# Attention and expert layer on one core: full rows in the middle slot's transfers, GpSimd's work in source order, table scatters a step behind the ranks

## The chip, the cores and the metric

The kernel runs on one core of one Trainium2 chip. The metric is device time in microseconds (us), the median of several executions. The engines are named as the profile names them: PE is TensorE (PEld its weight loads), DVE is VectorE, ACT is ScalarE, POOL is GpSimd, SP is SyncE, whose queue issues most DMAs. POOL issues the indirect ones.

## The reference

Eight batches of eight heads with 576 tokens each; the attention keeps only scores within `tau` of a row's maximum. Its output, 4608 tokens of 512 values, goes through a layer of eight experts, of which each token takes one.

```python
scores = scale * np.matmul(q, k.transpose(0, 1, 3, 2))        # q, k, v: (8, 8, 576, 64)
thresh = np.max(scores, axis=-1, keepdims=True) - tau
scores = np.where(scores >= thresh, scores, -1000000000.0)
attn = softmax(scores)                                        # sum + 1e-9
x = (attn @ v).transpose(0, 2, 1, 3).reshape(4608, 512)

logits = x @ w_gate + modality_bias[modality_id]
e_idx = np.argmax(logits, axis=1)
gate_w = softmax(logits)[range(N), e_idx]
for e in range(8):
    mask = e_idx == e
    h = np.maximum(x[mask] @ w1[e], 0.0)                      # w1[e]: 512 x 1024
    out[mask] = gate_w[mask, None] * (h @ w2[e])              # w2[e]: 1024 x 512
```

## The kernel before

Two heads make a pair; there are 32 pairs of nine steps each, one step for a tile of 128 queries (four tiles for each head, and one for the last 64 queries of both). In a step PE computes scores (L369), DVE takes the negated maximum `nm` (L386), ACT the exponentials `e` (L392), DVE the masked product `pr` (L404); two steps later PE transposes `pr` (L420), and later in the pair multiplies by `v` (L458).

Products of full precision are made of two parts each: an operand is split into a rounded part and the rest. `prep_steps` prepares the next pair in steps 0, 1 and 2 of a pair: PE transposes the remainder and the main rows of k and q (L294, L311), ACT copies them to `str` and `st` (L298, L299, L314), and POOL splits them in `split_pool` (a cast at L282, a subtraction at L283) into `nk`, `qb` and `nq`. SP then moves the halves to `km` (L320) and `q` (L323), from which the next pair's scores read. A weight block is loaded by SP into `raw` (four buffers; L771 for `w1`, L775 for `w2`) and split by POOL into `w1h`, `w1l` or `w2h`, `w2l` (L790 and L792; three buffers for `w1`, five for `w2`).

A "slot" is up to 512 tokens of one expert. Beside the attention run two slots of 256 and five of 512 (`SIDE`), each as soon as enough batches are done: `route_a` and `route_b` rank the tokens of a batch by expert, POOL scatters token number and gate weight to `tab` in five indirect DMAs (L617), `pick` chooses the expert, SP reads the slot's rows of the table to `tb` (L735), POOL gathers the tokens' rows to `xg` (L747), PE transposes them (L761) and computes the two layers (L805, L832), and POOL scatters the result `y` to the output (L847). After the attention follow slots for what is left (`last_slot`), in the sizes 512, 320 and 256; at least one of each of the two smaller ones always runs. The 320 are the "middle" size: two tiles of 128 rows and one of 64, `TP(t)` rows each.

Work is recorded step by step. `at(t, f)` puts a function at a step (fractions order them), `put(n, f)` behind a step's softmax, and the loop at L1053 runs them. The table `C` holds the places: for a 512-token slot, `wS`/`wL` give the steps of the weight splits, and each load stands `wl` = 3.5 steps ahead of its split. On PE the order recorded is the order run:

```python
    with tc.manual_schedule(engines={ET.PE}):
```

On the other engines a scheduler puts the instructions in an order of its own by modelled times; what stands in an engine's program then runs strictly in that order.

Of the kernel before, what the change touches and what calls it, by code (L numbers as in the profile page):

```python
# [11 lines left out]
F32 = mybir.dt.float32  # L12
# [3 lines left out]
U32 = mybir.dt.uint32  # L16
# [3 lines left out]
ET = mybir.EngineType  # L20
# [9 lines left out]
def tile_attn_moe(  # L30
# [11 lines left out]
    out: bass.AP,  # L42
):

    C = {'prep': [0, 1, 2], 'tr0': 6, 'pv0': 7, 'tr1': 12, 'sums': 13, 'pv1': 13, 'x': 14, 'gate': [15, 16, 17, 18], 'route': 18, 'routeb': 21, 'E0': 28, 'L0': 4, 'pick': -14, 'vld': 6, 'qkld': -3, 'pre': 2.5, 'wl': 3.5, 'rows': -11, 'gat': [-9.5, -8.5, -5, -4], 'xt': [-6, -5, -2, -1], 'lc': 21, 't3': 84, 'neg': 1.0, 'draw': [2, 2, 2, 2, 1, 2, 2, 1, 2], 'last': 36, 'te': 8, 'warm': 24,
         'wS': [-6, -4.7, -3.4, 3, 12.5, 14, 15.5, 21.5, 4.2, 5.4, 6.6, 7.5, 22.7, 23.8, 24.9, 25.8],
         'wL': [-5.5, -4, -2.5, 2.7, 12, 13.3, 14.6, 21, 3.8, 4.9, 6, 7.1, 15.8, 22.2, 23.4, 24.6], 'ask': 4, 'exp': -12.5, 'two': 98, 'early': []}
    nc = tc.nc
# [2 lines left out]
    DM = H * D  # L51
    DF = w1.shape[2]
    N = B * S
    P = 128
# [8 lines left out]
    W = 512  # L63
# [23 lines left out]
    xp = ctx.enter_context(tc.tile_pool(name="xp", bufs=1))  # L87
    actx = ctx.enter_context(ExitStack())
    ld = actx.enter_context(tc.tile_pool(name="ld", bufs=1))
    prep = actx.enter_context(tc.tile_pool(name="prep", bufs=1))  # L90
# [51 lines left out]
    warm = glob.tile([P, 1], F32, name="warm")  # L142
# [48 lines left out]
    xs = dram.tile([N, DM], F32, name="xs")  # L191
# [370 lines left out]


    prev_scatter = []

    def route_a(b):
        lg = state.pop(("lg", b))
# [20 lines left out]
    def route_b(b):  # L588
        l, oh = state.pop(("route", b))
        shp = [P, NT, NE]  # L590

        rk = tbank()
        rkv = rk[:, 0:(NT + 1) * NE].rearrange("p (t e) -> p t e", e=NE)
        mm(rkv, ltri, oh, True, False)
        for t in range(NT):
            mm(rkv[:, t + 1:NT + 1, :], ones_bf, oh[:, t:t + 1, :].to_broadcast([P, NT - t, NE]),
               False, t == NT - 1)

        nc.scalar.activation(out=l, in_=l, func=AF.Exp)
        pos = small.tile([P, NT + 1, NE], F32, name="pos", bufs=1)  # L600
        nc.vector.tensor_tensor(out=pos, in0=rkv, in1=base.unsqueeze(1).to_broadcast([P, NT + 1, NE]),
                                op=ALU.add)
        nc.vector.tensor_copy(out=base, in_=pos[:, NT, :])
        nc.vector.tensor_tensor(out=pos[:, 0:NT, :], in0=pos[:, 0:NT, :],
                                in1=creg.unsqueeze(1).to_broadcast(shp), op=ALU.add)
        nc.vector.tensor_tensor(out=pos[:, 0:NT, :], in0=pos[:, 0:NT, :], in1=oh[:, 0:NT, :], op=ALU.mult)
        posi = small.tile([P, NT], I32, name="posi")
        posf = small.tile([P, NT], F32, name="posf", bufs=1)
        nc.vector.tensor_reduce(out=posf, in_=pos[:, 0:NT, :], axis=AX.X, op=ALU.add)
        nc.vector.memset(posf[0:P - R, NC:NT], float(TROWS))  # L610
        nc.vector.tensor_copy(out=posi, in_=posf)
        gs = small.tile([P, NT], F32, name="gs", bufs=1)
        nc.vector.tensor_reduce(out=gs, in_=l, axis=AX.X, op=ALU.add)
        nc.vector.tensor_scalar(out=gs, in0=gs, scalar1=1e-9, scalar2=None, op0=ALU.add)
        nc.vector.reciprocal(out=pay[:, b, :, 1].bitcast(F32), in_=gs)
        for t in range(NT):
            i = _inst(nc.gpsimd.indirect_dma_start(  # L617
                out=tab, out_offset=bass.IndirectOffsetOnAxis(ap=posi[:, t:t + 1].bitcast(U32), axis=0),
                in_=pay[:, b, t, :], in_offset=None, bounds_check=TROWS - 1, oob_is_err=False))
            for o in prev_scatter:  # L620
                tc.declare_no_dep(i, o, reason="every token has a row of its own")
            prev_scatter.append(i)
# [91 lines left out]
    def slot(where, group, nrow, WT=W, wq=lambda: wp, nbuf=(4, 3, 5), lo_eng=None, xq=None):  # L714
# [3 lines left out]
        box = {}  # L718
# [3 lines left out]
        def TP(t):  # L722

            return min(P, WT - t * P)
# [17 lines left out]
        def gather(t):  # L742
            def f():
                xg = xt_pool().tile([P, DM], F32, name="xg", bufs=nx[1])
                box[("xg", t)] = xg

                nc.gpsimd.indirect_dma_start(  # L747
                    out=xg[0:TP(t)], out_offset=None, in_=xs[0:nrow, :],
                    in_offset=bass.IndirectOffsetOnAxis(ap=box["tb"][0:TP(t), t, 0:1].bitcast(U32), axis=0),
                    bounds_check=nrow - 1, oob_is_err=False)  # L750
            return f

# [68 lines left out]
        def l2(g, t, z):  # L821
            def f():
                if z == 0:
                    box["ps"] = group()
                nt = TP(t)
                ps = box["ps"]
                ts = slice(t * P, (t + 1) * P)
                f_ = g * F2 + z
                hh, hl = box[("h", f_)]
                wh, wl = box[("w", 2, f_)]  # L830
                for y, (h, w) in enumerate(((hh, wh), (hh, wl), (hl, wh))):
                    nc.tensor.matmul(out=ps, lhsT=h[:, ts], rhs=w, start=(z == 0 and y == 0),  # L832
                                     stop=(z == F2 - 1 and y == 2))
                if z < F2 - 1:
                    return
                let_go(ps)
                ps = ps[0:nt]
                tb = box["tb"][0:nt]
                if g == 0:
                    y0 = xp.tile([P, DM], F32, name="y0", bufs=W // P)[0:nt]  # L840
                    nc.scalar.activation(out=y0, in_=ps, func=AF.Copy, scale=tb[:, t, 1:2].bitcast(F32))
                    box[("y0", t)] = y0
                    return
                y = xp.tile([P, DM], F32, name="y", bufs=2)[0:nt]
                nc.vector.scalar_tensor_tensor(out=y, in0=ps, scalar=tb[:, t, 1:2].bitcast(F32),  # L845
                                               in1=box.pop(("y0", t)), op0=ALU.mult, op1=ALU.add)
                i = _inst(nc.gpsimd.indirect_dma_start(  # L847
                    out=out, out_offset=bass.IndirectOffsetOnAxis(ap=tb[:, t, 0:1].bitcast(U32), axis=0),
                    in_=y, in_offset=None, bounds_check=N - 1, oob_is_err=False))
                for o in prev_out:  # L850
                    tc.declare_no_dep(i, o, reason="every token has a row of its own")
                prev_out.append(i)
            return f
# [3 lines left out]
        ta = TT if xq else 0  # L857
        wl = C['wl']
        tb_ = ta + F2 * u1
# [9 lines left out]
        for f_ in range(FC):  # L869
# [3 lines left out]
            pre = C['pre'] if xq else C['pre'] * u1 / 2  # L873
# [28 lines left out]
    def at(t, f):  # L902
        events.setdefault(t, []).append(f)
# [32 lines left out]
    draw = [0] * (NSTEP + 2)  # L936
# [28 lines left out]
    for n0, (w, nb) in zip(begins, SIDE):  # L965
# [22 lines left out]
        for e in ev:  # L988

            if e[0] is None:  # L990
                t = n0 + e[2]
            elif n0 in begins[:-1]:

                which, f_ = e[3]
                t = n0 + C['w' + 'SL'[w == W]][8 * which + f_ - 8] - e[2]
            else:
                t = when(e[0]) - e[2]
# [24 lines left out]
        clear(fin["xp"], 4)  # L1022

    XF = NSTEP - NI + C['routeb'] + 1.5
    F0 = XF + 9.5
    at(XF, finish)

    def ask():
# [1 line left out]
    at(F0 + C['ask'], ask)  # L1030
    t0 = F0
    for z in range(3):
# [11 lines left out]
                f()  # L1044

    LAG = 2
    with tc.manual_schedule(engines={ET.PE}):

        ps = tbank()
        for _ in range(C['warm']):  # L1050
            nc.tensor.matmul(out=ps[:, 0:P], lhsT=zero, rhs=zero, start=True, stop=True, skip_group_check=True)
        prep_first(0)
        for n in range(NSTEP + LAG):  # L1053
            m = draw[n]
            if n == C['lc']:
                late_constants()
            if n == C['lc'] + 6:
                clear(xp, 2)
            two = 2 <= n < C['two']
            if n < NSTEP:  # L1060
                for hf in range(2):
                    qk_half(n, hf)
                softmax_a(n, two)
            if n == 0:
                prep_first(1)
            run_events(n - 0.5, n + 0.5)
            if two:
                if n % 2:
                    softmax_b(n - 1, two)
                    softmax_b(n, two)  # L1070
                if n >= LAG:
                    tr(n - LAG)
                if n % 2:
                    for y in (n - 1, n):
                        for f in extra.pop(y, []):
                            f()
                        pieces(draw[y])
                continue
            pieces(min(m, 1))
            if n < NSTEP:  # L1080
                softmax_b(n, two)
            if 0 <= n - LAG < NSTEP:
                tr(n - LAG)
            pieces(min(m - 1, 1))
            for f in extra.pop(n, []):
                f()
            pieces(m - 2)
# [48 lines left out]
```

## Time and profile before

| | |
|---|---|
| median of 3 runs | 1117.74 us (1115.88 to 1118.3) |
| the profiled execution | 1116.18 us |
| its span, first to last instruction | 1114.5 us |
| mean granted PE clock | 0.976 |
| busy: PE, DVE, ACT, POOL | 1029.7, 725.7, 641.9, 537.9 us |
| the last six score matmuls (L369) | from 887.08 us |

In a row of an engine's order of time stand start and duration in us, engine, line, operation, what it writes and reads, its shape, how many such instructions follow each other, and in brackets how long the engine stood idle before it, and what ended that. A row of a table of groups gives the busy time and the mean of one in ns.

### The profile page before, as it was taken

What the parts mean: (1) busy time and instruction counts of PE and PEld (TensorE: products, weight loads), DVE (VectorE), ACT (ScalarE), POOL (GpSimd) and SP (SyncE); (2) the same over time, 40 slices, a digit from 0 to 9 for tenths busy, and PEclk for the clock granted to TensorE, in tenths of its full rate; (3) what the DMA queues carried; (4) which work ended last, traced back from release to release, by engine and by line L of the source; (5) the groups of instructions that cost most, each with busy time, mean ns of one, the idle gap of its engine ahead of it and who ended that gap; (6) DMA issues with size and microseconds to landing.
All of it is one profiled execution on the core that took longest, in us unless ns stands there. A gap on an engine that the chain in (4) does not pass through costs nothing.

```text
span 1114.5 us, 20778 instructions
## 1 busy us (share of the span) xinstructions
PE 1029.7 (92%) x6683; PEld 809.9 (73%) x6683; DVE 725.7 (65%) x1773; ACT 641.9 (58%) x1474; POOL 537.9 (48%) x727
## 2 busy tenths in 40 slices
PE   7799869989798989999999999999999997999993
PEld 6676647777676767787777777777767775788883
DVE  6788857787568756876676766776677645243441
ACT  5687657666565656666666666566656523434440
POOL 2232345464655563665355644565265546442440
PEclk8999989999899999999999999999999999999997
DMA  5656557656666757476635763676465214644330
GB/s 123 140 136 160 124 128 184 165 110 165 165 161 130 180 129 184 102 202 162 168 82 141 197 161 91 148 206 147 107 141 152 97 39 134 216 145 131 131 99 21
DMA packets 212646, 156.06 MB, mean 140 GB/s; under 512 B 100782, under 2 KB 172462, under 8 KB 212528
## 3 DMA queue, kind: packets, MB, share of 16 engines
q1 hardware_dynamic: 205392, 135.72, 49.1%
q0 software_dynamic: 7136, 18.92, 5.2%
q8 instruction: 55, 0.90, 0.3%
q14 instruction: 63, 0.52, 0.1%
HBM read 84.12 MB, written 19.35 MB: 93 GB/s over the span
## 4 chain that ended last, share of the span: by engine, by line
PE 57%; DVE 3%; issue 2%; DMA 2%; ACT 1%; POOL 1%; another core or an unknown queue 0%; POOLq 0%; ACTq 0%; SPq 0%
PE bk L458 8%; PE bk L832 8%; PE bk L805 8%; PE s L369 8%; PE pm L832 7%; PE pm L805 6%; PE bk L420 6%; PE bk L761 1%; PE bk L311 1%; DVE pr L404 1%; PE bk L449 1%; DVE nm L386 1%; ACT e L392 1%; DMA xg<-xs,tb 1%; PE bk L507 1%
## 5 line engine op out<-in xcount | busy, mean ns | idle before, releaser
L386 DVE TENSOR_REDUCE nm<-s 128x1 f32<-128x576 f32 x288 | 216.9, 754 | 135.1 <-PE s L369 125.2
L392 ACT ACTIVATE e<-s,nm 128x576 f32<-128x576 f32 x288 | 215.0, 747 | 113.8 <-DVE nm L386 107.2
L404 DVE SCALAR_TENSOR_TENSOR pr<-s,nm,e 128x576 f32<-128x576 f32 x288 | 231.5, 815 | 75.1 <-ACT e L392 67.4
L369 PE MATMUL s<-km,q 128*128 128x288 f32 x1024 | 202.3, 320 | 41.1 <-DMA q<-nq 17.2
L431 ACT COPY ptm<-bk 128x512 f32<-128x512 f32 x256 | 149.3, 584 | 78.4 <-PE bk L420 66.4
L369 PEld LDWEIGHTS s<-km,q 128*128 128x128 f32 x1024 | 148.5, 192 | 62.1 <-issue 33.5
L420 PE MATMUL bk<-ident,pr 128*128 128x128 f32 x1152 | 175.8, 276 | 3.9 <-ACT ptm L431 2.0
L420 PEld LDWEIGHTS bk<-ident,pr 128*128 128x128 f32 x1152 | 143.6, 142 | 27.9 <-DVE hl L816 3.0
L458 PE MATMUL bk<-ptm,v_m 128*64 128x320 f32 (+1 forms) x1024 | 144.5, 420 | 0.1
L792 POOL TENSOR_TENSOR w2l<-raw,w2h 128x512 fp32r<-128x512 f32 x88 | 113.7, 1299 | 30.9 <-ACT w2h L788 26.7
L458 PEld LDWEIGHTS bk<-ptm,v_m 128*64 128x64 f32 x1024 | 67.6, 139 | 50.1 <-issue 10.3
L790 POOL CAST w2h<-raw 128x512 fp32r<-128x512 f32 x56 | 34.2, 613 | 140.1 <-DMA raw<-in_moe_w_dram 71.1
L433 ACT COPY rp<-pr 128x64 f32<-128x64 f32 x256 | 59.3, 248 | 56.5 <-DVE pr L404 47.0
L805 PE MATMUL bk<-xh,w1h 128*128 128x512 f32 (+1 forms) x212 | 85.5, 403 | 1.1 <-ACT xh L272 0.9
L805 PE MATMUL bk<-xl,w1h 128*128 128x512 f32 (+1 forms) x212 | 77.3, 365 | 1.9 <-DVE xl L273 1.9
L805 PE MATMUL bk<-xh,w1l 128*128 128x512 f32 (+1 forms) x212 | 76.9, 363 | 0.0
L747 POOL DMA_INDIRECT xg<-xs,tb x37 | 38.2, 1034 | 79.3 <-DMA tb<-tab 55.6
L832 PE MATMUL bk<-w2h,hh 128*128 128x512 f32 x176 | 75.7, 430 | 0.0
L847 POOL DMA_INDIRECT out_dram<-y,tb x37 | 38.6, 1042 | 74.4 <-DVE y L845 53.2
L792 POOL TENSOR_TENSOR w1l<-raw,w1h 128x512 fp32r<-128x512 f32 x56 | 71.8, 1285 | 2.9
L832 PE MATMUL bk<-w2h,hl 128*128 128x512 f32 x176 | 69.4, 394 | 0.0
L792 DVE TENSOR_TENSOR w1l<-raw,w1h 128x512 fp32r<-128x512 f32 x32 | 29.0, 908 | 61.5 <-ACT w1h L788 52.0
(205 smaller groups left out, 2006.7 us busy)
## 6 DMA issues: line engine op xcount, KB each, us to landing
raw<-in_moe_w_dram SPq DMA_DIRECT2D x176, 256.0 KB
q<-nq SPq DMA_DIRECT2D x124, 256.0 KB
km<-nk SPq DMA_DIRECT2D x124, 144.0 KB
v_m<-in_v_dram SPq DMA_DIRECT2D x32, 256.0 KB
xs<-xr SPq DMA_DIRECT2D x32, 256.0 KB
k_m<-in_k_dram SPq DMA_DIRECT2D x62, 128.0 KB
q_m<-in_q_dram SPq DMA_DIRECT2D x62, 128.0 KB
vr<-in_v_dram SPq DMA_DIRECT2D x64, 16.0 KB
```

Of the source, the lines that this page charges most:

```text
L369: nc.tensor.matmul(out=sps[:, hf, 0:SH], lhsT=a, rhs=x, start=(z == 0), stop=(z == len(passes) - 1))
L386: in_line(nc.vector.tensor_reduce(out=nm[:, 0:1], in_=sv, axis=AX.XY, op=ALU.max, negate=True), two)
L392: nc.scalar.activation(out=e, in_=sv, func=AF.Exp, bias=nm[:, 0:1])
L404: in_line(nc.vector.scalar_tensor_tensor(out=pr.rearrange("p (a x) -> p a x", a=2), in0=s2[n % 2][:, :, 0:SH], scalar=nm[:, 1:2], in1=e, o ...
L420: nc.tensor.transpose(out=ps[:, kc * P:(kc + 1) * P], in_=pr[:, kc * P:(kc + 1) * P], identity=ident)
L431: nc.scalar.copy(out=ptm[:, s, :, (c % 2) * P:(c % 2 + 1) * P], in_=pv)
L433: nc.scalar.copy(out=rp[:, i, :], in_=pr[:, SA:S])
L458: nc.tensor.matmul(out=o, lhsT=lhsT, rhs=rhs, start=start, stop=stop, skip_group_check=True)
L792: eng.tensor_tensor(out=lo, in0=raw, in1=hi.bitcast(F32), op=ALU.subtract)
L805: nc.tensor.matmul(out=ps[:, 0:WT], lhsT=a[:, cs], rhs=x[:, c, :], start=(c == 0 and z == 0), stop=(c == KC - 1 and z == 2))
L832: nc.tensor.matmul(out=ps, lhsT=h[:, ts], rhs=w, start=(z == 0 and y == 0), stop=(z == F2 - 1 and y == 2))
L847: i = _inst(nc.gpsimd.indirect_dma_start(out=out, out_offset=bass.IndirectOffsetOnAxis(ap=tb[:, t, 0:1].bitcast(U32), axis=0), in_=y, in_o ...
```

## The change

In its three parts: the attention's loop now names POOL beside PE as an engine whose order is that of the source; the five scatters to `tab` are taken out of `route_b` and placed one step after the step being recorded (`sc` = 1); and in slots whose size is no multiple of 128 the last gather, the results `y0` and `y` and their scatter take all 128 rows instead of 64. (`f0` only names a constant that stood in the code; the transposes of the gathered rows still take `TP(t)` rows.)

```diff
-    C = {... 'last': 36, 'te': 8, 'warm': 24,
+    C = {... 'last': 36, 'te': 8, 'f0': 9.5, 'sc': 1, 'warm': 24,
...
     prev_scatter = []
+    step = [0]
...
         nc.vector.reciprocal(out=pay[:, b, :, 1].bitcast(F32), in_=gs)
+        at(step[0] + C['sc'], lambda: scatter(b, posi))
+
+    def scatter(b, posi):
         for t in range(NT):
             i = _inst(nc.gpsimd.indirect_dma_start(
                 out=tab, out_offset=bass.IndirectOffsetOnAxis(ap=posi[:, t:t + 1].bitcast(U32), axis=0),
...
                 nc.gpsimd.indirect_dma_start(
-                    out=xg[0:TP(t)], out_offset=None, in_=xs[0:nrow, :],
-                    in_offset=bass.IndirectOffsetOnAxis(ap=box["tb"][0:TP(t), t, 0:1].bitcast(U32), axis=0),
+                    out=xg, out_offset=None, in_=xs[0:nrow, :],
+                    in_offset=bass.IndirectOffsetOnAxis(ap=box["tb"][:, t, 0:1].bitcast(U32), axis=0),
...
-                nt = TP(t)
...
-                ps = ps[0:nt]
-                tb = box["tb"][0:nt]
+                tb = box["tb"]
                 if g == 0:
-                    y0 = xp.tile([P, DM], F32, name="y0", bufs=W // P)[0:nt]
+                    y0 = xp.tile([P, DM], F32, name="y0", bufs=W // P)
...
-                y = xp.tile([P, DM], F32, name="y", bufs=2)[0:nt]
+                y = xp.tile([P, DM], F32, name="y", bufs=2)
...
-    F0 = XF + 9.5
+    F0 = XF + C['f0']
...
-    with tc.manual_schedule(engines={ET.PE}):
+    with tc.manual_schedule(engines={ET.PE, ET.Pool}):
...
             m = draw[n]
+            step[0] = n
```

The order of instructions changes on POOL and SP; on PE it stays, and on DVE and ACT it stays but for a few rows. The first place is POOL's order from the first batch's scatters on (128 to 161 us before). Before:

```order
L617 DMA tab<-pay,posi 37888x2 x5
L747 DMA xg<-xs,tb 128x512
L282 CAST nk_152<-str 128x64
L282 CAST qb_154<-str 64x64 x2
L283 TENSOR_TENSOR nk_152<-str,nk_152 128x64
L283 TENSOR_TENSOR qb_154<-str,qb_154 64x64 x2
L282 CAST nk_152<-st 128x512
L790 CAST w1h<-raw 128x512
L283 TENSOR_TENSOR nk_152<-st,nk_152 128x512
L792 TENSOR_TENSOR w1l<-raw,w1h 128x512
L790 CAST w1h<-raw 128x512
L747 DMA xg<-xs,tb 128x512
```

And now, on the same engine from the end of `nk`'s small splits to the second gather:

```order
L282 CAST nk_152<-st 128x512
L283 TENSOR_TENSOR nk_152<-st,nk_152 128x512
L282 CAST nq<-st 128x512
L283 TENSOR_TENSOR nq<-st,nq 128x512
L794 CAST w1h<-raw 128x512
L796 TENSOR_TENSOR w1l<-raw,w1h 128x512
L751 DMA xg<-xs,tb 128x512
L794 CAST w1h<-raw 128x512
L796 TENSOR_TENSOR w1l<-raw,w1h 128x512
L751 DMA xg<-xs,tb 128x512
```

Both gathers and the weight splits moved from before `nq` (which begins four rows below the piece shown) to behind it.

The second place is POOL's order from the first slot's result scatters on (268 to 299 us before). Before, with `nk_151`, `qb_153` and `nq` of the preparation:

```order
L790 CAST w2h<-raw 128x512
L792 TENSOR_TENSOR w2l<-raw,w2h 128x512
L282 CAST nk_151<-str 128x64
L283 TENSOR_TENSOR nk_151<-str,nk_151 128x64
L282 CAST qb_153<-str 64x64 x2
L847 DMA out_dram<-y,tb 4608x512
L283 TENSOR_TENSOR qb_153<-str,qb_153 64x64 x2
L790 CAST w2h<-raw 128x512
L792 TENSOR_TENSOR w2l<-raw,w2h 128x512
L282 CAST nk_151<-st 128x512
L283 TENSOR_TENSOR nk_151<-st,nk_151 128x512
L790 CAST w1h<-raw 128x512
```

Now:

```order
L849 DMA out_dram<-y,tb 4608x512 x2
L282 CAST nk_151<-str 128x64
L283 TENSOR_TENSOR nk_151<-str,nk_151 128x64
L282 CAST qb_153<-str 64x64
L283 TENSOR_TENSOR qb_153<-str,qb_153 64x64
L282 CAST qb_153<-str 64x64
L283 TENSOR_TENSOR qb_153<-str,qb_153 64x64
L282 CAST nk_151<-st 128x512
L283 TENSOR_TENSOR nk_151<-st,nk_151 128x512
L282 CAST nq<-st 128x512
L283 TENSOR_TENSOR nq<-st,nq 128x512
L794 CAST w1h<-raw 128x512
```

Before, three `w2` splits stood between the first result scatter and this preparation, a fourth and a `w1` split inside it; now all of them follow it.

The third place is SP's queue at the first slot of 512 tokens (390 to 416 us before; an `ISA` row sets the address of a load). Before:

```order
L775 DMA raw<-in_moe_w_dram 128x512
L771 ISA
L771 DMA raw<-in_moe_w_dram 128x4x128
L771 ISA
L771 DMA raw<-in_moe_w_dram 128x4x128
L113 DMA q_r<-in_q_dram 64x2x64
L113 DMA k_r<-in_k_dram 64x2x64
L771 ISA
L771 DMA raw<-in_moe_w_dram 128x4x128
L115 DMA k_m<-in_k_dram 128x4x64 x2
L320 DMA km_149<-nk_151 64x576 x4
L323 DMA q_147<-nq 64x2x512 x4
```

Now:

```order
L779 DMA raw<-in_moe_w_dram 128x512
L113 DMA q_r<-in_q_dram 64x2x64
L113 DMA k_r<-in_k_dram 64x2x64
L115 DMA k_m<-in_k_dram 128x4x64 x2
L320 DMA km_149<-nk_151 64x576 x3
L323 DMA q_147<-nq 64x2x512 x2
L320 DMA km_149<-nk_151 64x576
L323 DMA q_147<-nq 64x2x512 x2
L779 ISA
L779 DMA raw<-in_moe_w_dram 128x512
```

The three `w1` loads ahead of `km` and `q` are gone from there, and the fourth `w2` load comes behind `q`.

More of the change, by code (lines that the diff above doesn't have):

```diff
@@ L43, in tile_attn_moe @@
 ):
-    C = {'prep': [0, 1, 2], 'tr0': 6, 'pv0': 7, 'tr1': 12, 'sums': 13, 'pv1': 13, 'x': 14, 'gate': [15, 16, 17, 18], 'route': 18, 'routeb': 21, 'E0': 28, 'L0': 4, 'pick': -14, 'vld': 6, 'qkld': -3, 'pre': 2.5, 'wl': 3.5, 'rows': -11, 'gat': [-9.5, -8.5, -5, -4], 'xt': [-6, -5, -2, -1], 'lc': 21, 't3': 84, 'neg': 1.0, 'draw': [2, 2, 2, 2, 1, 2, 2, 1, 2], 'last': 36, 'te': 8, 'warm': 24,
+    C = {'prep': [0, 1, 2], 'tr0': 6, 'pv0': 7, 'tr1': 12, 'sums': 13, 'pv1': 13, 'x': 14, 'gate': [15, 16, 17, 18], 'route': 18, 'routeb': 21, 'E0': 28, 'L0': 4, 'pick': -14, 'vld': 6, 'qkld': -3, 'pre': 2.5, 'wl': 3.5, 'rows': -11, 'gat': [-9.5, -8.5, -5, -4], 'xt': [-6, -5, -2, -1], 'lc': 21, 't3': 84, 'neg': 1.0, 'draw': [2, 2, 2, 2, 1, 2, 2, 1, 2], 'last': 36, 'te': 8, 'f0': 9.5, 'sc': 1, 'warm': 24,
          'wS': [-6, -4.7, -3.4, 3, 12.5, 14, 15.5, 21.5, 4.2, 5.4, 6.6, 7.5, 22.7, 23.8, 24.9, 25.8],
```

## Prediction

> **What bounds the kernel now.** I read the page's busy times first, then the table of waits for TensorE (who waited for what: us in total, times, longest), then busy times in stretches, then TensorE's own rows in order of time; and from each gap found there, the rows of GpSimd (POOL), SyncE's queue (SP) and ScalarE (ACT) ahead of it.
>
> ```profile
> span 1114.5 us, 20778 instructions
> PE 1029.7 (92%) x6683; PEld 809.9 (73%) x6683; DVE 725.7 (65%) x1773; ACT 641.9 (58%) x1474; POOL 537.9 (48%) x727
> ...
> PE s L369 <- DMA q<-nq: 17.2, 3, 9.3
> ...
> 480.00:500.00 20.00, 20.00 (x133) 16.09 (x131) 14.41 (x32) 12.46 (x29) 14.87 (x20) 1.00 0.70 186
> ```
>
> TensorE is the bound: 92% busy, and full (20.00 us of 20) in a stretch of the steady part. There an earlier operand wins nothing; only TensorE's gaps can give time back. Its largest wait is that of L369, the scores, for the `q` transfer of the next pair of heads. The rows of these gaps, and busy times around the two long ones (after the stretch and its length: PE, PEld, DVE, ACT, POOL, then the granted clock):
>
> ```profile
> 165.66 1.30 PE L369 MATMUL s<-km,q 128*128 128x288 f32 x4 [9.27 <-DMA q<-nq]
> 271.63 0.77 PE L369 MATMUL s<-km,q 128*128 128x288 f32 x4 [1.09 <-issue]
> 303.13 1.30 PE L369 MATMUL s<-km,q 128*128 128x288 f32 x4 [7.65 <-DMA q<-nq]
> 417.16 0.77 PE L369 MATMUL s<-km,q 128*128 128x288 f32 x4 [3.17 <-issue]
> ...
> 160.00:165.60 5.60, 0.00 (x0) 0.00 (x0) 0.00 (x0) 0.00 (x0) 0.64 (x1) 0.50 0.64 141
> 166.00:170.00 4.00, 4.00 (x19) 2.51 (x19) 2.67 (x7) 1.44 (x3) 0.00 (x0) 0.54 0.81 195
> 303.00:306.00 3.00, 2.87 (x13) 2.90 (x14) 1.53 (x4) 0.68 (x2) 0.00 (x0) 0.50 0.92 201
> ```
>
> All four are the first scores of a pair. From 160 to 165.6 us TensorE, VectorE and ScalarE all stand at 0.00: nobody works ahead during the stall, so what it loses comes back whole. Behind the two long stalls the granted clock is 0.54 and 0.50, and the same four matmuls take 1.30 instead of 0.77.
>
> **Part 1: GpSimd in source order.** What stood before the first stall:
>
> ```profile
> 142.03 0.35 ACT L299 ACTIVATE str<-bk,gq 128x64 f32<-128x64 f32 x1
> 146.51 0.69 ACT L314 ACTIVATE st<-bk,gq 128x512 f32<-128x512 f32 x1
> ...
> 144.21 1.05 POOL L747 DMA_INDIRECT xg<-xs,tb  x1 [8.93 <-DMA tb<-tab]
> 148.80 0.24 POOL L282 CAST qb<-str 64x64 fp32r<-64x64 f32 x1 [3.11 <-DMA xg<-xs,tb]
> 158.69 0.61 POOL L282 CAST nq<-st 128x512 fp32r<-128x512 f32 x1
> 159.37 1.26 POOL L283 TENSOR_TENSOR nq<-st,nq 128x512 fp32r<-128x512 f32 x1
> ...
> 160.66 3.46 SPq L323 DMA_DIRECT2D q<-nq  x4
> ...
> 169.65 0.66 PE L761 MATMUL bk<-ident,xg 128*128 128x128 f32 x4
> ```
>
> ScalarE had the `st` of q ready at 147.20 (146.51 + 0.69), but GpSimd began to split it at 158.69: it had stood 8.93 for a gather's table, 3.11 for that gather's landing, and then had three weight splits and a second gather ahead of `nq`. In the new order the chain holds no gather and no weight split. `str` is there at 142.38; the small splits of `nk` and `qb` take some 2 us, the large one of `nk` as long as one of `nq`, 1.9; so GpSimd is free at about 146.3, begins `nq` with `st` at 147.2 and ends at 149.1. SP issues four transfers in 3.46, to 152.6. From the end of that issue (164.12) to the first matmul (165.66) it was 1.54, so q is there at about 154.2; TensorE asked at 156.39 (165.66 less 9.27). The stall goes, with 2 us to spare. What is late next? The two gathers now issue at about 151 and 154, behind one weight split each; the first one of before was landed 4.6 us after its issue (144.21 to 148.80), which puts the second near 159, against a use (L761, 169.65) that comes 4 us behind the first scores, so at 160 to 161. Nearly a tie: up to 1 us, left to the range.
>
> The second and the third stall:
>
> ```profile
> 280.33 0.69 ACT L314 ACTIVATE st<-bk,gq 128x512 f32<-128x512 f32 x1
> 274.27 0.75 DVE L845 SCALAR_TENSOR_TENSOR y<-bk,tb,y 128x512 f32<-128x512 f32 x1
> 280.30 0.61 POOL L790 CAST w2h<-raw 128x512 fp32r<-128x512 f32 x1 [10.41 <-DMA raw<-in_moe_w_dram]
> 297.00 1.26 POOL L283 TENSOR_TENSOR nq<-st,nq 128x512 fp32r<-128x512 f32 x1
> 298.29 3.42 SPq L323 DMA_DIRECT2D q<-nq  x4
> ...
> 394.51 0.70 ACT L314 ACTIVATE st<-bk,gq 128x512 f32<-128x512 f32 x1
> 406.04 0.32 POOL L283 TENSOR_TENSOR qb<-str,qb 64x64 fp32r<-64x64 f32 x1 [3.31 <-DMA out_dram<-y,tb]
> 410.96 1.28 POOL L283 TENSOR_TENSOR nq<-st,nq 128x512 fp32r<-128x512 f32 x1
> ```
>
> Second: a weight split that stood 10.41 for its load, and four more, came ahead of a `st` that was ready at 281.02; `nq` ended at 298.26. Now only the two result scatters stand ahead, and the later `y` is ready at 275.02. Each issue takes 1 us; with 4 us for the landing, which `qb` waits for (3.31 in the row of the third), and 4.5 us of splits, `nq` ends near 285, and q lands near 290.3 (3.42 of issue and the 1.54). TensorE asks at 295.48 (303.13 less 7.65): 5 us to spare. Third: `st` is ready at 395.21, so `nq` ends between 397 and 399 and q lands by 404, needed at 413.99. The 1.09 at 271.63 is of the same kind, and its `nq` moves ahead of two weight splits; I count it whole.
>
> Stalls: 9.27 + 7.65 + 3.17 + 1.09 = 21.2 us. Clock: 4.00 x 0.46 = 1.84 behind the first, 2.87 x 0.50 = 1.44 behind the second, 3.3 together. Sum 24.5 us.
>
> [...] The row at 417.16 is at full speed, so I leave the third out.
>
> What hides the weight splits, now behind the preparation? Rows of a steady slot:
>
> ```profile
> 563.71 0.61 POOL L790 CAST w2h<-raw 128x512 fp32r<-128x512 f32 x1 [17.04 <-PE bk L832]
> 576.33 1.28 POOL L283 TENSOR_TENSOR nq<-st,nq 128x512 fp32r<-128x512 f32 x1
> 580.01 0.99 POOL L617 DMA_INDIRECT tab<-pay,posi  x1 [2.40 <-DVE pk_r L632]
> 585.14 0.97 POOL L617 DMA_INDIRECT tab<-pay,posi  x1 [0.30 <-issue]
> 599.46 0.48 PE L832 MATMUL bk<-w2h,hh 128*128 128x512 f32 x1
> ...
> POOL w2h L790 <- DMA raw<-in_moe_w_dram: 71.1, 14, 14.0
> ```
>
> Three `w2` splits, done by 569.5 before, move behind the scatters: 586.1 + 3 x 1.9 = 591.8, against the use of the first of them at 599.46, where TensorE takes its second piece. Some 7.6 us are left, so they cost nothing; late loads would use that up (a rival below). The gather, which stood 8.93 right behind the scatters, now stands in the next preparation, and GpSimd splits weights meanwhile. On SP the loads move with their splits: ahead of the third stall four `w2` and three `w1` loads stood before the pair's `km` and `q` transfers, now three `w2` loads do and the rest comes behind. That takes them out of q's way; they wait for the same buffers as before, so I cost the move at nothing.
>
> **Part 2: scatters a step later.** Nothing is added, 5 scatters stay 5. They are tied to a place in the order, not to a clock: by the rows above GpSimd stood 2.40 for the ranks anyway. The cost lies between 0 and one `w1` split put ahead of them, 1.9. I take 0, since who waits for them is SP's read of `tb` and then the gathers, and these now stand in the next preparation and not right behind the scatters.
>
> **Part 3: full rows.** One 320-row slot runs here:
>
> ```profile
> 994.34 0.96 POOL L747 DMA_INDIRECT xg<-xs,tb  x1 [0.33 <-PE bk L761]
> ...
> L841 ACT ACTIVATE y<-pm,tb 128x512 f32<-128x512 f32 x12 | 8.3, 688 | 16.7 <-PE pm L832 16.7
> L841 ACT ACTIVATE y<-pm,tb 64x512 f32<-64x512 f32 x1 | 0.7, 685 | 0.1
> ```
>
> Its gather of 64 rows issues in 0.96, a full one (144.21) in 1.05; an activation of 64 partitions takes 685 ns, of 128 688. Together about 0.1 us, beside matmuls: 0. The 64 rows more hold no token and move nothing.
>
> **Sum.** This execution took 1116.18, 1.68 beyond its span. 1116.18 - 24.5 = 1091.7. The runs' median, 1117.74, is 1.56 above it: 1093.
>
> **The rivals.** (a) More: VectorE's ranking and choice of expert run free of GpSimd's splits.
>
> ```profile
> 230.56 0.15 DVE L628 SCALAR_TENSOR_TENSOR pk_a<-done,base 1x8 f32<-1x8 f32 x1
> 232.58 1.28 POOL L283 TENSOR_TENSOR nq<-st,nq 128x512 fp32r<-128x512 f32 x1
> 234.55 1.22 DVE L637 SCALAR_TENSOR_TENSOR done<-pk_a,done 1x8 f32<-1x8 f32 x1
> 238.13 0.69 PE L449 MATMUL bk<-ident,rp 128*128 128x128 f32 x2 [3.85 <-ACT ptm L431]
> ```
>
> A 1x8 operation takes 0.15 or 1.22, the long ones beside GpSimd's splits; behind this chain TensorE stands 3.85. In the new order GpSimd would wait at its scatter at that time. That could free the 3.85 and a slow clock like the others' (1.6): 1087.5. Against it: ScalarE's copies and the softmax in VectorE's queue remain. [...]
>
> (b) Less: q is split early, but SP, whose queue is in order, stands before a weight load for which no buffer is free, so that only the first stall goes, 9.27 + 1.84: 1106.6. For it: the loads wait for buffers that GpSimd's splits free, and those now come later. Against it: the fourth `w2` load and the `w1` loads now stand behind q.
>
> (c) Slower: in the five steady slots the `w2` splits come late. It decides at the 7.6 us above. A load late by the longest wait of the table, 14.0, gives 6.4 each: 5 x 6.4 - 24.5 = +7.5, 1125. Against it: the loads are placed 3.5 steps ahead of their splits, some 11 us (four pairs, 36 steps, lie between the gaps at 303.13 and 417.16).
>
> (d) It does nothing, since the transfers themselves are late: 1117. Against it: `st` lay ready for 11 to 16 us.
>
> **How the numbers follow.** Forecast 0.50 (its own range 1089 to 1099), (a) 0.14, (b) 0.18, (c) 0.12, (d) 0.06. Faster by over 0.2%, about what a measurement of this kernel can tell from no change: 0.82; same 0.06; slower 0.12. The range runs from (a) less 2 to (b) plus 5: 1085 to 1112.
>
> **What would show it.** Right: no gap over 2 us before first scores at L369 between 150 and 420 us; each `nq` split within 2 us of its `st`; the clock at 1.00 there; no GpSimd wait for `tb` right behind the scatters. Wrong: TensorE waiting for `w1`, `w2` or `xg` in the steady part (c), or for `q` as before (b, d).

## The result, and the profile after

The changed kernel takes 1074.63 us (median of 4 runs, 1071.42 to 1077.13), the kernel before 1117.24 beside it (4 runs, 1115.88 to 1118.3): a ratio of 0.9618, 95% interval 0.9582 to 0.9653. That is 42.6 us less. The forecast was 24.5 us less, 1093, and its range ended at 1085: right in direction, wrong by 18 us. The profiled execution took 1077.08, its span is 39.2 us shorter.

The head of the page, and of the table of TensorE's waits (us in total, times, longest), of the changed kernel:

```profile
span 1075.3 us, 20759 instructions
PE 1025.0 (95%) x6683; PEld 808.1 (75%) x6683; DVE 716.1 (67%) x1773; ACT 640.5 (60%) x1474; POOL 540.9 (50%) x727
```

```profile
PE s L369 <- DVE pr L404: 13.7, 20, 2.5
...
PE bk L294 <- DMA q_r<-in_q_dram: 1.6, 1, 1.6
```

TensorE does the same 6683 matmuls. The scores' wait for `q`, 17.2 us before, is not in the table; a new one of 1.6 for `q_r` is. Where the 39.2 us lie is seen by taking the same matmul (counted from the first) in both traces:

| matmul | before | after | earlier by | gained since the row above | what stands there in before |
|---|---|---|---|---|---|
| 960 | 148.16 | 147.09 | 1.07 | 1.07 | start |
| 1080 | 175.28 | 166.53 | 8.75 | 7.68 | the q stall of 9.27 and the slow clock behind it |
| 1440 | 224.71 | 215.51 | 9.20 | 0.45 | |
| 1560 | 245.56 | 232.37 | 13.19 | 3.99 | the 3.85 behind the choice of expert |
| 1800 | 280.80 | 266.98 | 13.82 | 0.63 | the q stall of 1.09 |
| 1920 | 304.87 | 282.38 | 22.49 | 8.67 | the q stall of 7.65 and its slow clock |
| 2640 | 412.47 | 389.90 | 22.57 | 0.08 | |
| 2760 | 434.93 | 408.95 | 25.98 | 3.41 | the q stall of 3.17 |
| 3840 | 600.24 | 573.37 | 26.87 | 0.89 | 1.35 behind a batch's ranking |
| 4560 | 710.76 | 682.76 | 28.00 | 1.13 | 1.24 behind a batch's ranking |
| 5400 | 842.31 | 810.25 | 32.06 | 4.06 | 1.96 behind a batch's ranking, and a slow clock |
| 6682, the last | 1096.65 | 1066.61 | 30.04 | -2.02 | the slots after the attention |
| end of the span | 1114.46 | 1075.27 | 39.19 | 9.15 | behind the last matmul |

So the four q stalls gave 7.68 + 0.63 + 8.67 + 3.41 = 20.4 us (forecast with the clock: 24.5), four places behind a batch's ranking 3.99 + 0.89 + 1.13 + 4.06 = 10.1, the end of the program 9.15, and the rest -0.4.

What answers to the rows ahead of the first stall, from the timeline of the changed kernel:

```profile
145.44 0.69 ACT L314 ACTIVATE st<-bk,gq 128x512 f32<-128x512 f32 x1
146.19 0.61 POOL L282 CAST nq<-st 128x512 fp32r<-128x512 f32 x1 [1.08 <-ACT st L314]
146.88 1.28 POOL L283 TENSOR_TENSOR nq<-st,nq 128x512 fp32r<-128x512 f32 x1
148.10 0.61 POOL L794 CAST w1h<-raw 128x512 fp32r<-128x512 f32 x1
...
150.22 1.07 POOL L751 DMA_INDIRECT xg<-xs,tb  x1
...
148.19 3.72 SPq L323 DMA_DIRECT2D q<-nq  x4
...
156.27 0.62 SPq L113 DMA_DIRECT2D q_r<-in_q_dram  x1
160.01 0.24 PE L294 MATMUL bk<-ident,q_r 64*128 64x64 f32 x1 [1.60 <-DMA q_r<-in_q_dram]
```

GpSimd now waits for `st` (1.08) instead of `st` for GpSimd (11.49 before), and `q` is issued by 151.91, where the forecast had 152.6. The new wait is for the rest of q of the pair after: SyncE issued that load at 156.27, behind the loads of v.

The choice of expert for the first of these four places, on VectorE, and GpSimd beside it:

```profile
222.32 0.22 DVE L637 TENSOR_SCALAR pk_a<-iota,pk_r 1x8 f32<-1x8 f32 x1
222.85 0.14 DVE L641 SCALAR_TENSOR_TENSOR done<-pk_a,done 1x8 f32<-1x8 f32 x1
...
220.81 1.28 POOL L796 TENSOR_TENSOR w1l<-raw,w1h 128x512 fp32r<-128x512 f32 x1
222.48 1.05 POOL L621 DMA_INDIRECT tab<-pay,posi  x1 [0.39 <-DVE pk_r L636]
```

The update of `done`, 1.22 us in before, takes 0.14: GpSimd issues scatters there and splits nothing. (One 1x8 operation of that chain, at 221.27, still takes 0.84 beside a split.)

And the end of the program. These are groups of GpSimd's sequencer (how often: duration least/median/longest in ns, first and last start in us), before in the first fence, after in the second:

```profile
L1102 POOLq INC_SWDGE_SEM  x1: 2468/2468/2468, 1101.7 to 1101.7; - x1
L1132 POOLq DRAIN  x3: 40/107/9375, 1104.2 to 1114.2; - x3
```

```profile
L1105 POOLq INC_SWDGE_SEM  x1: 348/348/348, 1073.3 to 1073.3; - x1
L1135 POOLq DRAIN  x3: 40/107/718, 1073.7 to 1075.0; - x3
```

Behind its last scatter (to 1099.10 in before) GpSimd jumps over the conditional slots, raises DMA semaphores at their line (`INC_SWDGE_SEM`, from 1101.74), and drains (from 1104.24 to 1113.62); the last semaphore instructions of all engines, 1113.7 to 1114.4, come behind that drain. It took 9.38 us and takes 0.72; the raising took 2.47 and takes 0.35. No engine has a row of other work beside it: in before 17.81 us lie between the start of the last matmul and the end, now 8.65.

### The profile page after: what moved, and what is told of

Its sections match the earlier page's. It is cut to its first block, busy times and chain, and to the rows that moved or that the text cites. A ratio compares the mean times of both kernels' runs of the same rounds, so it can differ in the third digit from the quotient of the medians.

```text
span 1075.3 us, 20759 instructions
## 1 busy us (share of the span) xinstructions
PE 1025.0 (95%) x6683; PEld 808.1 (75%) x6683; DVE 716.1 (67%) x1773; ACT 640.5 (60%) x1474; POOL 540.9 (50%) x727
## 3 DMA queue, kind: packets, MB, share of 16 engines
q0 software_dynamic: 7200, 18.92, 5.4%
## 4 chain that ended last, share of the span: by engine, by line
PE 81%; DVE 8%; issue 4%; DMA 3%; ACT 2%; POOL 1%; SPq 0%; POOLq 0%; DVEq 0%; ACTq 0%
PE s L369 15%; PE bk L458 14%; PE bk L809 11%; PE bk L835 10%; PE bk L420 10%; PE pm L835 6%; PE pm L809 5%; DVE pr L404 3%; DVE nm L386 3%; PE bk L311 2%; PE bk L765 2%; PE bk L449 1%; PE bk L507 1%; ACT e L392 1%; PE bk L539 1%
## 5 line engine op out<-in xcount | busy, mean ns | idle before, releaser
L369 PE MATMUL s<-km,q 128*128 128x288 f32 x1024 | 200.8, 318 | 19.4 <-DVE pr L404 13.1
L369 PEld LDWEIGHTS s<-km,q 128*128 128x128 f32 x1024 | 147.6, 191 | 39.6 <-DVE pr L404 21.3
L282 POOL CAST nk<-str 128x64 fp32r<-128x64 f32 x31 | 7.4, 240 | 239.4 <-ACT str L298 230.1
L458 PEld LDWEIGHTS bk<-ptm,v_m 128*64 128x64 f32 x1024 | 67.2, 138 | 50.5 <-issue 10.1
L835 PE MATMUL bk<-w2l,hh 128*128 128x512 f32 x176 | 69.0, 392 | 0.0
```

What stands on the lines that cost most here:

```text
L369: nc.tensor.matmul(out=sps[:, hf, 0:SH], lhsT=a, rhs=x, start=(z == 0), stop=(z == len(passes) - 1))
L458: nc.tensor.matmul(out=o, lhsT=lhsT, rhs=rhs, start=start, stop=stop, skip_group_check=True)
```

## Experiments: which part gave what

First the three parts apart.

**GpSimd in source order, and nothing else** (run 1).

```diff
-    with tc.manual_schedule(engines={ET.PE}):
+    with tc.manual_schedule(engines={ET.PE, ET.Pool}):
```

> Before, with GpSimd's order taken from the source and nothing else: the scatters stay in the step of the ranks, the middle slot keeps its 64-row pieces. Theory A (the order of the splits is the whole change): within 0.3% of the changed kernel, 1071 to 1078 us, the four q stalls gone. Rival B (without the later scatters GpSimd stands at its scatter for the ranks, and what is behind it in its queue comes late): seven batches of 2 to 4 us, some of it shown as TensorE waits behind the routing: 1085 to 1100 us. Of the end of the program: in before GpSimd's last drain took 9.38 us and in the changed kernel 0.72; if the new order is the cause, it is under 1 us here, if the full rows are the cause, it is 9 us and the time is 1080 to 1087.

1087.2 us against 1118.92 of before, ratio 0.9709 (0.9675 to 0.9743). The q stalls and the 3.85 behind the choice are gone from TensorE's waits; the drain is 9375 ns as in before. So the order alone gives some 32 us, and theory A's 1071 to 1078 is missed. The time lies where rival B's and that of the full rows meet. The long drain speaks for the latter, but something of B is there too: TensorE stands for `xr` behind the ranking of four batches, 1.03 to 1.73 us each. The row of its table of waits, in run 1 first, then in the changed kernel:

```profile
PE bk L449 <- DVE xr L510: 4.9, 4, 1.7
```

```profile
PE bk L449 <- DVE xr L510: 1.1, 2, 0.9
```

**The scatters one step later, GpSimd still scheduled** (run 2).

```diff
+        at(step[0] + C['sc'], lambda: scatter(b, posi))      # sc = 1
```

> Before, with the scatters written one step later, GpSimd still placed by the scheduler, 64-row pieces kept. Theory A (the order is the whole change): same as before, 1112 to 1122 us, the stalls of 9.27 and 7.65 us at the scores still there. Rival B (the place of the scatters is what holds nq): the stalls shrink by the 2.4 us that GpSimd stands for the ranks and more, 1100 to 1110 us. GpSimd's last drain: about 9 us if the order is what shortens it.

1118.35, ratio 1.0001 (0.9981 to 1.0021): nothing, as theory A says. The two long stalls and the 3.85 stand about as before (the third stall, of 3.17, is not there, since TensorE comes to it 3.2 us later):

```profile
PE s L369 <- DMA q<-nq: 16.1, 3, 8.2
PE bk L449 <- ACT ptm L431: 3.9, 1, 3.9
```

**Full rows alone** (run 3).

```diff
-                    out=xg[0:TP(t)], out_offset=None, in_=xs[0:nrow, :],
+                    out=xg, out_offset=None, in_=xs[0:nrow, :],
...
-                y = xp.tile([P, DM], F32, name="y", bufs=2)[0:nt]
+                y = xp.tile([P, DM], F32, name="y", bufs=2)
```

> Before, with full rows in the middle slot alone. Theory A: same as before, 1115 to 1120 us, GpSimd's last drain still about 9 us. Rival C (the full rows are what shortens the end of the program): 9 us less, 1106 to 1110 us, and a drain under 1 us.

1108.03, ratio 0.9902 (0.9872 to 0.9932): 10.9 us, and the drain is short:

```profile
L1135 POOLq DRAIN  x3: 40/107/718, 1105.1 to 1106.4; - x3
```

The last matmul stands 1.6 us *later* than in before, so all of it lies behind that.

**The changed kernel with 64-row pieces** (run 4).

```diff
-                    out=xg, out_offset=None, in_=xs[0:nrow, :],
+                    out=xg[0:TP(t)], out_offset=None, in_=xs[0:nrow, :],
...
-                y = xp.tile([P, DM], F32, name="y", bufs=2)
+                y = xp.tile([P, DM], F32, name="y", bufs=2)[0:nt]
```

> The changed kernel with the 64-row pieces of before in the middle slot. Theory A: same as the changed kernel, 1071 to 1078 us, drain under 1 us. Rival C (full rows shorten the end): 1080 to 1087 us, drain about 9 us.

1084.5, ratio 0.9685 (0.9655 to 0.9716), drain 9375 ns: rival C, from the other side. Beside the order alone (0.9709) the times cannot tell what the later scatters are worth, since the intervals overlap. The traces can: from matmul 2400 to matmul 5760 run 1 gains 5.8 us on before, and the twelve profiles with the order and the scatters of the changed kernel, whatever their rows, gain 9.2 to 9.6 (runs 4 to 7, 9, 10, 13 to 16, 18 and the changed kernel itself). In the new order the later scatters give about 3.5 us there, though by themselves they give nothing.

## Experiments: what the full rows do

**Only the slot that runs** (run 5)**, or only the copies that are jumped over** (run 6).

```diff
-                    out=xg, out_offset=None, in_=xs[0:nrow, :],
+                    out=xg[0:(P if skip else TP(t))], out_offset=None, in_=xs[0:nrow, :],   # the other way: TP(t) if skip else P
```

> The changed kernel, but the middle slot that always runs has its 64-row pieces again (the gather and the result scatter of its third tile); the copies of that slot in the conditional part at the end, which is jumped over here, keep full rows. Rows alone in the middle slot took GpSimd's increment of the DMA semaphores at the conditional part from 2.47 to 0.35 us and its last drain from 9.38 to 0.72. Theory D1 (a DMA of fewer than 128 rows that was executed leaves that to the end): 2.47 and 9.38 again, one run at 1080 to 1087 us. Theory D2 (it is made up at the jump for the 64-row DMAs that are jumped over): 0.35 and 0.72, one run at 1070 to 1078 us.

> The counterpart: full rows in the middle slot that runs, 64-row pieces only in the conditional copies that are jumped over. D1: 0.35 and 0.72 us, one run at 1070 to 1078 us. D2: 2.47 and 9.38, 1080 to 1087 us.

Short pieces in the slot that runs: 1085.16, 2468 and 9375 ns. In the jumped-over ones: 1073.77, 348 and 718 ns. What was executed counts, not what is jumped over.

**Only the gather short** (run 7).

```diff
-                    out=xg, out_offset=None, in_=xs[0:nrow, :],
+                    out=xg[0:TP(t)], out_offset=None, in_=xs[0:nrow, :],
```

> The changed kernel with 64 rows in the middle slot's gathers alone, in the copy that runs and in those jumped over; its result scatters stay full. If each 64-row DMA has its share in the 8.66 us: a drain of about 5 us and half of the 2.12 more at the semaphores. If one short DMA of any kind sets off the whole: 9.38 and 2.47. If the scatter alone does it: 0.72 and 0.35.

1081.97, 2468 and 9375 ns: one short gather brings the whole. That looked like "any short DMA sets it off", and the next two asked for it.

**More gathers**, into a buffer that nobody reads, behind the gathers of the first slot after the attention (runs 9 and 10, then 13 to 15; run 16 leaves one out instead):

```diff
+                for r in [P] if first and t == TT - 1 else []:       # or [64] * 4, [64], [P] * 8
+                    xz = xt_pool().tile([P, DM], F32, name="xg", bufs=nx[1])
+                    nc.gpsimd.indirect_dma_start(out=xz[0:r], ...)
```

> The changed kernel with one more gather of 128 rows, into a buffer that nobody reads, behind the gathers of the first slot after the attention: 115 indirect DMAs of 128 rows instead of 114. It costs some us in that slot; what is asked is the end. D1 (any executed DMA of fewer than 128 rows sets off the long end): 0.35 us at the semaphores and a drain of 0.72. D2' (the sum of the rows must fill a block, 256 by what was seen: 14592 rows gave the short end, 14464 and 14528 the long one): 14720 rows, so 2.47 and 9.38.

> The same with four more gathers of 64 rows in that place, 256 rows more, so 14848, again a multiple of 256. D1: 2.47 and 9.38. D2': 0.35 and 0.72.

368 and 800 ns with one of 128 rows; 388 and 882 ns with four of 64 (one run each, 1072.7 and 1080.11; the four delay that slot by some 6 us). The short DMAs did *not* bring the long end, so D1 fell; the 14720 rows did not either, so "a full block of 256" fell too. What was left is the mere sum of rows:

> The changed kernel with the 64-row pieces of before (two short DMAs, 14464 rows) and one more gather of 128 rows, that nobody reads, behind the gathers of the first slot after the attention: 14592 rows, the sum that had the short end with full rows. Theory T (the end depends on how many rows GpSimd's DMAs have moved, and is long below 14592): 0.35 to 0.4 us at the semaphores and a drain of 0.72. Theory U (two short DMAs among full ones leave the long end, whatever the sum): 2.47 and 9.38.

> The changed kernel with one more gather of 64 rows in that place: 14656 rows, one short DMA, the sum above 14592 and no multiple of 128. T: short, 0.35 to 0.4 and 0.72. U (a short DMA that is not made up to a full block behind it): 2.47 and 9.38.

> The changed kernel with eight more gathers of 128 rows in that place, 15616 rows; the slot gets some 10 to 20 us longer. T as a bound: short. T as a place in a ring that comes round within 1024 rows: the answer of 14592, short; of another length: it may be long, 2.47 and 9.38.

> The changed kernel with one gather of 128 rows left out, the last of the first slot after the attention; its tile is filled with zeros instead, so that the results of its tokens are not computed. All DMAs are of 128 rows, their sum is 14464, as with the two short ones. T: long, 2.47 and 9.38. U: short, 0.35 and 0.72.

One run each, 1077.57, 1074.49, 1085.4 and 1085.99 us. All four as theory T says (run 15: short, though its drain is 1.372). Runs 13, 14 and 15 have the gathers of the diff above, 13 with the 64-row pieces of before besides; run 16 has, for one gather:

```diff
+                if first and t == TT - 1:
+                    nc.vector.memset(xg, 0.0)
+                    return
```

Without any short DMA it is long:

```profile
L1113 POOLq INC_SWDGE_SEM  x1: 2448/2448/2448, 1071.6 to 1071.6; - x1
L1143 POOLq DRAIN  x3: 40/107/9293, 1074.1 to 1084.0; - x3
```

All kernels by the sum of rows (us):

| kernel | indirect DMAs | rows | at the semaphores | last drain | last matmul to end |
|---|---|---|---|---|---|
| run 16 | 113 | 14464 | 2.45 | 9.293 | 17.63 |
| before | 114 | 14464 | 2.47 | 9.375 | 17.81 |
| run 7 | 114 | 14528 | 2.47 | 9.375 | 17.93 |
| changed | 114 | 14592 | 0.35 | 0.718 | 8.65 |
| run 13 | 115 | 14592 | 0.35 | 0.718 | 8.73 |
| run 14 | 115 | 14656 | 0.35 | 0.718 | 8.77 |
| run 9 | 115 | 14720 | 0.37 | 0.800 | 7.21 |
| run 10 | 118 | 14848 | 0.39 | 0.882 | 7.17 |
| run 15 | 122 | 15616 | 0.51 | 1.372 | 7.78 |

Over these kernels the drain rises, falls once and rises again. It takes 0.082 us for each indirect DMA (113 to 114: 9.293 to 9.375), falls to 0.718 with the DMA that reaches an edge, and grows by 0.082 again for each one behind that (1, 2 and 8 of them: 0.800, 0.882, 1.372). The edge lies above the 14528 rows of run 7 and at 14592 at most. The changed kernel has exactly 14592: its 128 rows more put the very last DMA on that edge.

The account does not fall to nothing there. All rows of the table fit one line, 0.065 + 0.08167 n for the drain and 0.188 + 0.020 n at the semaphores, where n is the number of all DMAs if the edge is not reached, and 8 plus the DMAs behind it if it is. So "begins anew" in the next text means a start from eight; what these eight are is not shown.

**The test of it: before, plus one useless gather** (run 17). The edit of run 9, in before.

> Before, untouched in its order and its 64-row pieces, with one more gather of 128 rows that nobody reads, behind the gathers of the first slot after the attention: 14592 rows instead of 14464. Theory T (GpSimd's last drain takes 0.082 us for each indirect DMA since its count began, and the count begins anew where 14592 rows are reached): a drain of 0.72 instead of 9.38 and 0.35 at the semaphores instead of 2.47, some 9 us less behind the last matmul, 1106 to 1112 us, although the kernel does more. Rival (the short end needs full rows in before's order): 1116 to 1121 us, 9.38.

1107.92 against 1117.59, ratio 0.9922 (0.9893 to 0.9951): before becomes 9.7 us faster by one gather more, as much as by full rows.

```profile
L1113 POOLq INC_SWDGE_SEM  x1: 348/348/348, 1102.9 to 1102.9; - x1
L1143 POOLq DRAIN  x3: 40/107/718, 1103.3 to 1104.5; - x3
```

**And in the changed kernel**, behind the last slot's gathers (run 18):

> The changed kernel with one more gather of 128 rows behind the last slot's gathers. In the changed kernel the 14592nd row comes with the very last DMA, and from the last matmul to the end it took 8.65 us; with one or four more DMAs 7.2. By T the drain is 0.80 and the end 7.2, 1.4 us less than the changed kernel, 1069 to 1077 us, within its spread. Rival (the gather delays the last slot's splits): 1076 to 1080 us.

1074.7, ratio 0.9610 (0.9561 to 0.9658), not to be told from the changed kernel's 0.9618; the drain is 800 ns and the end 7.11 us as expected. The 1.5 us between 8.65 and 7.11 lie ahead of the last scatter: in the changed kernel, where the sum reaches the edge with it, it stood 3.29 us (1.80 in before); here, where the sum reaches it with the one before, it stands 0.34.

```profile
1069.55 0.99 POOL L849 DMA_INDIRECT out_dram<-y,tb  x1 [3.29 <-issue]
```

```profile
1069.40 0.98 POOL L860 DMA_INDIRECT out_dram<-y,tb  x1 [0.34 <-DVE y L858]
```

## Experiments: VectorE beside GpSimd, and the rest of the first stall

**Scatters three steps behind the ranks** (run 8), so that weight splits come ahead of them again:

```diff
-'sc': 1
+'sc': 3
```

> The changed kernel with the table scatters three steps behind the ranks instead of one: in every steady slot one or two weight splits that stood behind the five scatters now stand ahead of them, so that GpSimd splits weights while VectorE chooses the next expert. Theory A' (part of the gain came from VectorE's ranking and choosing beside an idle or issuing GpSimd; in before its 1x8 operations took up to 1.26 us beside splits, in the changed kernel 0.14 to 0.22): some of these operations are over 0.8 us again, TensorE waits 1 to 4 us for ptm behind them in several of the five slots, 1077 to 1086 us. Rival (only the q splits count): 1071 to 1077 us, no such wait.

1078.28, ratio 0.9646 (0.9616 to 0.9676). The interval overlaps the changed kernel's, but the place tells it:

```profile
222.43 1.27 DVE L637 TENSOR_SCALAR pk_a<-iota,pk_r 1x8 f32<-1x8 f32 x1
224.36 1.22 DVE L641 SCALAR_TENSOR_TENSOR done<-pk_a,done 1x8 f32<-1x8 f32 x1
...
222.39 1.28 POOL L796 TENSOR_TENSOR w2l<-raw,w2h 128x512 fp32r<-128x512 f32 x1
224.30 1.26 POOL L796 TENSOR_TENSOR w2l<-raw,w2h 128x512 fp32r<-128x512 f32 x1
...
227.93 0.69 PE L449 MATMUL bk<-ident,rp 128*128 128x128 f32 x2 [3.47 <-ACT ptm L431]
```

Each of the two 1x8 operations starts and ends within 0.06 us of a two-input split on GpSimd, and TensorE stands 3.47 behind them: the 3.85 of before is back, and this matmul comes 2.95 us later than in the changed kernel, counted from matmul 1440.

Behind three more batches (at 444.49, 563.18 and 681.85) TensorE stands 1.06 to 1.10 for `ptm`, and 0.6 to 0.9 us each came back. That fits the expectation's numbers, but not its mechanism: one 1x8 operation of each batch took 1.03, but 9 us ahead of the wait (553.86 against 563.18), and VectorE stood idle in between. So it was in before: the ranking that stands from 577 us on there ended at 581.72, and the operation for which TensorE waits at 587.98 had itself stood for TensorE. The rows of this batch, in before, in run 1 and in the changed kernel:

```profile
583.55 0.60 PE L507 MATMUL bk<-ident,ot 128*128 128x128 f32 x4
585.14 0.97 POOL L617 DMA_INDIRECT tab<-pay,posi  x1 [0.30 <-issue]
587.23 0.69 DVE L510 TENSOR_TENSOR xr<-bk,ri 128x512 f32<-128x512 f32 x1 [2.26 <-PE bk L522]
587.98 0.44 PE L449 MATMUL bk<-ident,rp 128*128 128x128 f32 x2 [1.35 <-DVE xr L510]
```

```profile
558.25 0.60 PE L507 MATMUL bk<-ident,ot 128*128 128x128 f32 x4
559.53 0.98 POOL L617 DMA_INDIRECT tab<-pay,posi  x1 [0.30 <-issue]
561.68 0.69 DVE L510 TENSOR_TENSOR xr<-bk,ri 128x512 f32<-128x512 f32 x1 [2.27 <-PE bk L522]
562.43 0.44 PE L449 MATMUL bk<-ident,rp 128*128 128x128 f32 x2 [1.10 <-DVE xr L510]
```

```profile
557.62 0.60 PE L507 MATMUL bk<-ident,ot 128*128 128x128 f32 x4
558.84 0.69 DVE L510 TENSOR_TENSOR xr<-bk,ri 128x512 f32<-128x512 f32 x1
559.66 0.98 POOL L621 DMA_INDIRECT tab<-pay,posi  x1 [0.30 <-issue]
561.93 0.58 ACT L431 COPY ptm<-bk 128x512 f32<-128x512 f32 x1 [2.87 <-PE s L369]
562.57 0.66 PE L420 MATMUL bk<-ident,pr 128*128 128x128 f32 x4 [0.41 <-ACT ptm L431]
```

`xr` is made of what L507 wrote. VectorE begins it 3.08 us behind the end of L507 in before, 2.83 in run 1 and 0.62 in the changed kernel. At all these places VectorE or ScalarE, idle until then, begins 1.1 to 1.3 us behind the end of the batch's last scatter: in before at 587.23, 706.40 and 824.34 (ends at 586.11, 705.09, 823.16), in run 1 at 561.68, in run 8 at 562.55, and in the changed kernel at 561.93, where it costs TensorE 0.41. So what these places cost seems to hang on where the five scatters fall among TensorE's matmuls. That is read from the rows alone; why the other engines go on that late is not shown by any run.

**The loads of q and k earlier**, by one step (run 11) and by two (run 12):

```diff
-'qkld': -3
+'qkld': -4      # and -5
```

> The changed kernel with the loads of the next pair's q and k asked one step earlier. In its profile TensorE stood 1.60 us for q_r at 160.01, since SyncE issued that load at 156.27 behind the loads of v, and the clock was 0.56 behind it from 160 to 163. If that late load is what is left of the first stall: the 1.60 and some 1.3 us of slow clock go, 1069 to 1075 us. Rival (the load only changes places with those of v, and TensorE waits for these or for a buffer instead): 1072 to 1079 us.

> The same two steps earlier. If earlier is simply better: as with one step, 1069 to 1075 us. Rival: SyncE, in order, stands for a buffer of k or q that the running preparation still reads, and the transfers of q behind it come late: a wait of the scores for q of 1 us or more, 1075 to 1090 us.

1076.97 and 1077.95, ratios 0.9634 (0.9587 to 0.9681) and 0.9638 (0.9581 to 0.9694): no gain that shows. With one step the wait for `q_r` is gone and matmul 1080 stands 3.1 us better against matmul 960, but waits for `xr` came: 2.56 at 325.83, 1.91 at 442.31 with a slow clock behind it, and 1.92 at 563.44. With two steps there are two of them, 2.46 and 1.92. The expected wait for q did not come in either.

## Why the prediction was right, and why it was wrong

**Right: part 1's q stalls.** There is no gap over 0.9 us before first scores at L369 between 150 and 420 us. `nq` is split 0.06 us after its `st` in most of the 31 pairs and at most 2.6 after (15.1 in before). The promise of 2 us was narrowly missed, with no wait behind it. No scatter is followed by a wait for `tb` until the end of the attention (900.22, 5.58). Rivals (b), (c) and (d) are out: no wait over 0.4 us for `w1`, `w2` or the `q` of the scores in the steady part.

**Wrong: "Part 3: ... Together about 0.1 us, beside matmuls: 0."** It is 9.15 us in the profiles and 10.9 by the times of the run with full rows alone. I priced what the 64 rows more cost where they are issued. I never read the rows behind the last matmul, where the profile of before showed 17.8 us with a drain of 9.38 in it; a view of that stretch would not have told what sets the drain, but it would have given the range its lower end.

**Wrong: rival (a) as an alternative, at a chance of 0.14.** It is a consequence of the same order (run 1 has 4.22 at its place), so it adds to the forecast instead of standing against it. It gave 3.99 there; its own working had 3.85 and 1.6. The split that it showed beside `done` (232.58) had ended at 233.86, before `done` began at 234.55; the one that stood against it is

```profile
234.49 1.26 POOL L792 TENSOR_TENSOR w1l<-raw,w1h 128x512 fp32r<-128x512 f32 x1
```

And I looked at one batch. The places behind three more gave 6.1, not by this chain (above), and the prediction has nothing on them.

**Mis-sized: part 2, "I take 0".** The later scatters measure 0 by themselves (run 2), but in the new order about 3.5 us, outside the 0 to 1.9 that they were costed at, and the other way: a gain. They are most of those 6.1: in the same three rows of the table run 1 has -0.5, 0.5 and 2.3 where the changed kernel has 0.9, 1.1 and 4.1.

**Mis-sized: the first stall with its clock.** Forecast 9.27 + 1.84 = 11.1, measured 7.68. "What is late next?" had only the gathers; it was the load of `q_r`, which moved to behind the loads of v: 1.60, and then one stretch of slow clock. That stretch is chance: of the twelve profiles named above five have one there and gain 6.3 to 7.7, seven have none and gain 8.5 to 9.5. The wait for `q_r` is in all twelve (1.27 to 2.99); without it, in runs 11 and 12, the gain is 10.8. So in the profile the term "the clock at 1.00 there" failed as well:

```profile
156.94:160.35 3.41, 1.81 (x15) 1.01 (x12) 3.15 (x10) 2.38 (x7) 0.00 (x0) 1.00 0.81 221
160.00:163.00 3.00, 2.98 (x15) 2.92 (x16) 0.98 (x5) 1.01 (x3) 1.60 (x6) 0.56 0.85 259
```

Summed: 20.4 for 24.5 at the stalls, 10.1 for 0, 9.15 for 0, -0.4 elsewhere: 39.2 in the span. The profiled execution of the changed kernel lies 2.45 above its median, that of before 1.06 below its own, which makes it 42.6.

## What to carry to other kernels

Read the stretch behind the last matmul as closely as the longest gap: here nothing overlaps, and 9 us hung on a sum of DMA rows. When an engine's queue is put in another order, list every engine that shares something with what was moved: the transfer that waited for it, and the neighbour that stood against it. Two such effects add; they are not rivals. And where a table names the engine that ended a wait, look whether that engine was busy or stood itself.

## What the runs showed of the hardware

GpSimd's last drain took 9.293 us behind 113 indirect DMAs of the whole program and 9.375 behind 114, 0.082 for one more, and 0.718, the price of eight, where their rows reached an edge between 14528 and 14592. Behind the edge it grew by 0.082 a DMA, to 1.372 at 15616 rows (run 15); whether it comes round again farther on was not tried. The bytes that moved hardly differ: 18.92 MB on GpSimd's queue in before and in the changed kernel, in 7136 and 7200 packets. The runs changed the sum by rows of 2 KB alone, so whether the rows or the bytes that were asked for are counted is open.

The granted clock changes on a fixed grid of 3.41 us: in the profiles of before and of the changed kernel it stayed at one value for 3.41, 6.83, 10.24 us or a larger multiple each time, but for the last, which the end cuts off. And a stretch need not be idle to halve the next one. Taken over the twenty profiles, from 45 us to 1055 us: of 47 such stretches at full clock with TensorE busy for under 40% all were followed by half clock; of 92 between 40 and 60% 19 were; of 82 between 60 and 70% one; of 5575 over 70% none. In the profiles of before and of the changed kernel alone it is 4 of 4, 6 of 12, none of 9 and none of 548. The 1.81 us busy of 3.41 above is one of the 19. The changed kernel's own runs differ by 5.7 us, from 1071.42 to 1077.13. That slow stretches make the difference is an estimate from two profiles: run 6 (1073.77), whose executed slots are the same, had one behind 45 us (0.83 from 900 to 920), where the profile above (1077.08) has four.
